# Score tiles 0 and 1 in one pair of PSUM banks, reciprocals transposed from 128 columns, and their 1e-9 added by GpSimd

## The chip, the cores and the metric

One core of a Trainium2 chip. The metric is the time of one execution on the device in microseconds, the median of a few runs. Another 0.5% (some 5 us) is about what a measurement of this kernel can tell from no change.

## The reference, cut to what matters

An attention with forgetting gates feeds two feed-forward networks. Only the attention is touched: batch 4, 8 heads, 576 positions, 64 values a head.

```python
scores = scale * np.matmul(q, k.transpose(0, 1, 3, 2))
cum = np.cumsum(np.log(np.clip(f, 0.0001, 1.0)), axis=-1)
scores = np.where(causal, -1e9, scores + cum[:, :, :, None] - cum[:, :, None, :])
attn = np.exp(scores - np.max(scores, axis=-1, keepdims=True))
attn = attn / (np.sum(attn, axis=-1, keepdims=True) + 1e-09)
x = np.matmul(attn, v)
```

## The kernel before

The work of the attention goes by pairs of heads, 16 of them. Every product is made of two fp32r parts (h and l) of each factor. The steps of a pair `p`, with their engines:

- `load_q`, `load_k`, `load_v`, `decay_rows`: DMAs of SyncE. `qh`, `kh`, `ql`, `kl`, `v_high`, `v_low`: GpSimd makes the two parts.
- `scores` i (TensorE, i = 0 to 4): the score tiles of 128 rows, four terms each. Tiles 0 to 3 use 64 rows of the array for each head, both heads side by side, each head into a bank of its own (tag "s", two banks in all); a tile of fewer than 256 columns is made 256 wide. Tile 4 has both heads in one tile on 128 rows (tag "X").
- `minimum` t (VectorE, t = 0 to 8, tile i and 8 - i being the two heads of score tile i): reads the scores from PSUM, adds the mask, writes them to the tile P and gives the row's extreme. `exp` t (ScalarE): the exponential in place, with the row's sum.
- `transposes` g (TensorE, g = 0 to 6): 25 blocks of P, two to four in a bank (tag "t", two banks in all). `evac_h` g (ScalarE) and `evac_l` g (VectorE) take the two parts out.
- `rinv` (VectorE): adds 1e-9 to the nine sums of a row (line 280) and takes the reciprocal (line 281). `rinv_t` (TensorE, also tag "t") transposes the nine columns, `rinv_b` (ScalarE) copies them out, `rinv_c` and `rinv_d` (SyncE) send them to DRAM and spread them over the partitions.
- `pv` (TensorE, line 324), `out_a` (ScalarE), `out_b` (VectorE), `out_c` (GpSimd, times the reciprocal), `out_d` (SyncE).

The order is written out by hand. `WHEN` gives each step a due time in units of a plan; pair p adds 9 p to it, the first pair uses `START` and the last `END`; `run` sorts all steps by due time and emits them in that order, and every engine executes its own in the order of emission. So the order on an engine is read by taking the due times modulo 9. A tile's buffer is reused in the order in which the tiles are made: the next tile waits until the readers of the one before in that buffer are done. Between the steps stand those of `Weights.op` (list `STEPS`), which prepare the weights of the next layer: one in three or fewer units on VectorE (`SHIFT`, `LOW`, `SIGN`), most of them at 3.294 modulo 9, from the middle on some at 6.381. After the attention come the two networks, in which TensorE has no idle time that matters.

Modulo 9 the parts of the order that the change meets are, before it:

- TensorE: `pv` 0 4, 0 3, 0 1, 1 0, 1 2, `scores` 1, `transposes` 2, 3, `pv` 1 4, 1 3, 1 1, `scores` 0, `rinv_t`, `transposes` 5, 4, `scores` 2, `pv` 0 0, `scores` 4, `pv` 0 2, `transposes` 6, `scores` 3, `transposes` 0, 1.
- VectorE: `minimum` 3, 5, `rinv`, `evac_l` 0, 1, `minimum` 1, 7, a step of `Weights`, `evac_l` 2, 3, `minimum` 0, 8, `out_b` 0, 1, `minimum` 6, `evac_l` 5, `minimum` 2, `evac_l` 4, `minimum` 4, `evac_l` 6.
- ScalarE: `evac_h` 0, 1, `exp` 3, 5, `out_a` 0, `evac_h` 2, 3, `out_a` 1, `rinv_b`, `exp` 7, `evac_h` 5, 4, `exp` 0, 1, 4, 2, `evac_h` 6, `exp` 6, 8.

Of the kernel before, what the change touches and what calls it, by code (L numbers as in the profile page):

```python
# [9 lines left out]
F32 = mybir.dt.float32  # L10
# [3 lines left out]
ALU = mybir.AluOpType  # L14
# [7 lines left out]
class Attention:  # L22
# [59 lines left out]
    def constants(self):  # L82

        nc, c, S = self.nc, self.c, self.S
        self.qrs = [c.tile([128, 640], F32, name=f"qr{i}") for i in range(2)]
        for q in self.qrs:
            nc.gpsimd.memset(q[0:64, 576:640], 0.0)
            nc.gpsimd.memset(q[64:128, 512:576], 0.0)
        self.nbs = [c.tile([128, S], F32R, name=f"nb{i}") for i in range(2)]
        nc.gpsimd.memset(self.nbs[0][64:128].bitcast(F32), 0.0)  # L90

        self.one = c.tile([128, 256], F32R, name="one")
        o = self.one[:].bitcast(F32)
        nc.gpsimd.memset(o, 0.0)
        for r, t in ((0, 128), (64, 192)):
            nc.gpsimd.memset(o[r:r + 2, 0:128], 1.0)
            nc.gpsimd.memset(o[r:r + 2, t:t + 64], 1.0)

        self.mask = c.tile([128, 512], F32, name="mask")
        nc.gpsimd.memset(self.mask, 0.0)  # L100
        nc.gpsimd.affine_select(self.mask, self.mask, pattern=[[-1, 512]], compare_op=ALU.is_ge,
                                fill=-8e9, base=384, channel_multiplier=1)
        self.mask4 = c.tile([128, S], F32, name="mask4")
        self.eps = c.tile([128, 9], F32, name="eps")
        nc.gpsimd.memset(self.eps, 1e-9)

    def constants2(self):
        nc, c, S = self.nc, self.c, self.S
        nc.gpsimd.memset(self.mask4, 0.0)
        for i in range(2):  # L110
            M = self.mask4[64 * i:64 * i + 64]
            nc.gpsimd.affine_select(M, M, pattern=[[-1, S]], compare_op=ALU.is_ge, fill=-8e9, base=512,
                                    channel_multiplier=1)
        nc.gpsimd.memset(self.nbs[1][:].bitcast(F32), 0.0)
        ident = c.tile([128, 128], F32, name="ident")
        nc.gpsimd.memset(ident, 0.0)
        nc.gpsimd.affine_select(ident, ident, pattern=[[-1, 128]], compare_op=ALU.not_equal,
                                fill=1.0, base=0, channel_multiplier=1)
# [74 lines left out]
    def v_low(self, R, p):  # L193
        self.sub(("v_low",), R["V"][:, :, :, 1], R["vr"].rearrange("p j (h e) -> p j h e", h=2), R["V"][:, :, :, 0])

    def scores(self, R, p, i):


        nc, S = self.nc, self.S
        Xh, Xl, Yh, Yl, nb = R["Xh"], R["Xl"], R["Yh"], R["Yl"], self.nbs[p % 2]  # L200
        if "P" not in R:
            R["P"] = self.pp.tile([128, sum(self.W9)], F32, tag="P", name=f"P{p}")
            R["m"] = self.sm.tile([128, 9], F32, tag="m", name=f"m{p}")
            R["sum"] = self.sm.tile([128, 9], F32, tag="sum", name=f"sum{p}")
        n = 4
        if i == 4:
            ps = self.ps.tile([128, 1024], F32, tag="X", name=f"s{p}_4")
            for c in range(2):
                for j, (L, r) in enumerate(((Xh[:, 512:640], Yh), (Xl[:, 512:640], Yh), (Xh[:, 512:640], Yl),
                                            (self.one[:, 128:256], nb))):  # L210
                    nc.tensor.matmul(ps[:, 224 + 288 * c:512 + 288 * c], L, r[:, 288 * c:288 * c + 288],
                                     start=j == 0, stop=j == n - 1)
            R["src", 4] = R["P"], ps[:, 224:800], self.mask4
            return
        w = self.W9[i]
        N = max(w, 256)
        ps = [self.ps.tile([128, 512], F32, tag="s", bufs=2, name=f"s{p}_{i}_{h}") for h in range(2)]
        q = slice(128 * i, 128 * i + 128)
        for j, (L, r) in enumerate(((Xh[:, q], Yh), (Xl[:, q], Yh), (Xh[:, q], Yl), (self.one[:, 0:128], nb))):
            for h in range(2):  # L220
                o = slice(64 * h, 64 * h + 64)
                nc.tensor.matmul(ps[h][:, 0:N], L[o], r[o, 0:N], start=j == 0, stop=j == n - 1)  # L222
        for h in range(2):
            R["src", (i, 8 - i)[h]] = R["P"], ps[h][:, 0:w], self.mask[:, 512 - w:512]

    def minimum(self, R, p, t):
        P, src, mask = R["src", t]
# [46 lines left out]
            self.nc.vector.tensor_sub(l, s, h)  # L274


    def rinv(self, R, p):
        nc = self.nc
        r = self.sm.tile([128, 9], F32, tag="r", name=f"r{p}")
        nc.vector.tensor_add(r, R["sum"], self.eps)  # L280
        nc.vector.reciprocal(r, r)
        R["r"] = r

    def rinv_t(self, R, p):
        ps = self.ps.tile([128, 512], F32, tag="t", bufs=2, name=f"rt{p}")
        self.nc.tensor.transpose(ps[0:9, 0:128], R["r"], self.ident)
        R["rt"] = ps

    def rinv_b(self, R, p):
# [54 lines left out]
    def out_d(self, R, p):  # L344
# [13 lines left out]
        ("load_q",): -23.5799, ("load_k",): -16.9757, ("qh",): -11.2698, ("kh",): -9.873, ("ql",): -9.3162,  # L358
        ("kl",): -9.0904, ("decay_rows",): -8.1126, ("scores", 4): -2.7503, ("scores", 3): -2.135,
        ("minimum", 4): -2.019, ("minimum", 3): -0.0192, ("minimum", 5): 0.3552, ("scores", 1): 2.0404,  # L360
        ("exp", 3): 2.9766, ("exp", 5): 3.066, ("minimum", 1): 3.0798, ("minimum", 7): 3.2918, ("scores", 0): 4.02,
        ("minimum", 0): 4.7488, ("minimum", 8): 4.7664, ("exp", 7): 4.9241, ("scores", 2): 5.5069,
        ("minimum", 6): 5.8865, ("exp", 0): 6.2356, ("minimum", 2): 6.379, ("exp", 1): 6.6423, ("exp", 4): 6.7033,
        ("exp", 2): 7.105, ("transposes", 0): 7.5695, ("load_v",): 7.7728, ("exp", 6): 7.8053,
        ("transposes", 1): 7.9929, ("exp", 8): 8.7191, ("evac_h", 0): 9.5166, ("evac_h", 1): 9.5706,
        ("rinv",): 10.083, ("v_high",): 10.1126, ("evac_l", 0): 10.4436, ("v_low",): 10.514,
        ("evac_l", 1): 11.2219, ("transposes", 2): 12.2269, ("evac_h", 2): 12.276, ("transposes", 3): 12.3519,
        ("evac_h", 3): 12.4099, ("evac_l", 2): 13.0431, ("rinv_t",): 13.1193, ("rinv_b",): 13.2113,
        ("evac_l", 3): 13.7368, ("transposes", 5): 13.8096, ("transposes", 4): 13.9726, ("evac_h", 5): 14.8574,
        ("pv", 0, 0): 14.9016, ("evac_h", 4): 14.9515, ("evac_l", 5): 15.137, ("pv", 0, 2): 15.291,  # L370
        ("evac_l", 4): 15.6663, ("transposes", 6): 15.699, ("evac_h", 6): 16.5991, ("evac_l", 6): 16.839,
# [3 lines left out]
        ("out_b", 0): 22.9328, ("out_b", 1): 23.1796, ("out_c",): 27.9509, ("out_d",): 29.0433}  # L375
    START = {
        ("scores", 1): -93.1054, ("minimum", 7): -76.489, ("minimum", 1): -61.3588, ("load_v",): -51.5282,
        ("scores", 4): -51.4691, ("scores", 0): -44.2927, ("minimum", 4): -43.1442, ("minimum", 0): -42.9929,
        ("exp", 1): -39.9503, ("minimum", 8): -34.2473, ("exp", 4): -33.3442, ("scores", 2): -33.1312,
        ("minimum", 6): -32.9417, ("minimum", 2): -30.1161, ("exp", 0): -27.5664, ("v_high",): -26.4226,  # L380
        ("exp", 8): -25.5812, ("scores", 3): -25.0262, ("exp", 7): -15.5786, ("exp", 6): -14.3123,
# [4 lines left out]
        ("evac_l", 0): 4.0423, ("evac_l", 5): 4.5113, ("transposes", 6): 6.9606, ("evac_h", 6): 7.9405,  # L386
        ("transposes", 2): 8.6556, ("evac_h", 2): 9.5839, ("pv", 0, 0): 10.1568, ("pv", 0, 4): 10.8868,
        ("evac_l", 6): 11.2953, ("evac_l", 2): 12.6569, ("transposes", 4): 13.0223, ("pv", 0, 2): 13.1329,
        ("evac_h", 4): 13.5619, ("rinv",): 13.795, ("evac_l", 4): 14.2703, ("rinv_t",): 15.9595,
        ("rinv_b",): 16.8417, ("pv", 0, 3): 18.6967, ("pv", 0, 1): 19.0591, ("rinv_c",): 19.3907,  # L390
        ("pv", 1, 0): 19.9842, ("pv", 1, 4): 20.0606, ("pv", 1, 3): 20.5574, ("pv", 1, 2): 21.0619,
        ("pv", 1, 1): 21.6901, ("out_a", 0): 22.1074, ("out_a", 1): 22.8142, ("out_b", 0): 22.9613,
# [3 lines left out]
        ("kl",): -7.3377, ("ql",): -3.7962, ("load_v",): -3.2787, ("scores", 4): -2.3475, ("minimum", 4): -2.1479,  # L396
        ("scores", 3): -1.8482, ("minimum", 5): 0.0327, ("minimum", 3): 0.4621, ("exp", 5): 0.5894,
        ("exp", 4): 2.234, ("scores", 1): 2.774, ("minimum", 1): 2.8564, ("minimum", 7): 3.1801,
        ("scores", 0): 4.1802, ("minimum", 8): 5.1018, ("exp", 3): 5.8442, ("minimum", 0): 5.8642,
        ("scores", 2): 6.4249, ("exp", 1): 6.5503, ("exp", 7): 7.1358, ("minimum", 6): 7.8256, ("exp", 6): 8.5445,  # L400
        ("minimum", 2): 10.9888, ("exp", 0): 12.1987, ("exp", 2): 12.2247, ("transposes", 0): 14.1161,
        ("evac_h", 0): 14.7614, ("exp", 8): 14.8228, ("transposes", 2): 15.3451, ("evac_l", 0): 15.8926,
        ("v_high",): 16.9288, ("evac_h", 2): 17.1908, ("transposes", 1): 18.0963, ("evac_h", 1): 18.3091,
        ("evac_l", 2): 19.0513, ("rinv",): 19.0903, ("transposes", 4): 19.1493, ("evac_l", 1): 19.2978,
        ("rinv_t",): 22.2139, ("evac_h", 4): 22.6115, ("rinv_b",): 24.2699, ("evac_l", 4): 25.904,
        ("rinv_c",): 27.1176, ("v_low",): 27.3115, ("transposes", 3): 27.4876, ("evac_h", 3): 29.2544,
        ("transposes", 5): 29.4306, ("evac_l", 3): 31.4099, ("evac_h", 5): 32.5541, ("transposes", 6): 32.9931,
# [142 lines left out]
class Moe1:  # L550
# [12 lines left out]
    def hidden(self, u, pieces):  # L563
        nc, ch, W = self.nc, self.chain, self.W
        t, fc = divmod(u, self.FC)
        N = self.TILES[t][1]
        (wh, wl), (xh, xl) = self.W.done[f"wi{fc}"], self.x.parts[t]
        ph = self.ps.tile([128, 512], F32, tag="s", bufs=2, name=f"h{u}")[:, 0:N]
        three(nc, ph, [(block(wh, c), block(wl, c), xh[:, c], xl[:, c]) for c in range(4)], True, True)
# [566 lines left out]
```

## Time and profile before

| | |
|---|---|
| median of 3 runs | 1052.52 us (1050.94 to 1055.83) |
| span of the profiled execution | 1054.0 us |
| TensorE, VectorE, ScalarE, GpSimd busy, share of the span | 97%, 64%, 43%, 14% |
| the attention's steady part, pairs 3 to 15 | 44.31 to 189.02 us |

The profiled execution lies 1.5 us over the median and within the runs. A timeline's row gives the start in us from the start of the span, the length in us, the engine, the line of the kernel, the operation, the tiles it writes and reads, shapes, and how many like it follow one another; in brackets stands how long the engine was idle before and who ended that.

### The profile page before, as it was taken

The page shows a single profiled execution, that of the slowest core. Times are in us where ns is not written, and L with a number is a line of the kernel's source. Part 1 is how long each engine was busy: PE and PEld are TensorE (multiplying, and loading weights), DVE is VectorE, ACT ScalarE, POOL GpSimd, SP SyncE. Part 2 cuts the span into 40 slices and gives each one's busy share as a digit, 9 for nine tenths or more (in the row PEclk, how much of TensorE's full clock was granted, in tenths as well). Part 3 has the DMA queues.
Part 4 walks back from the last instruction along what each step waited for, and adds up shares of the span by engine and source line. Part 5 has one row for each costly group of instructions (what it writes and reads, how often), then busy time and mean ns, then how long its engine had stood idle before and what let it go on. Part 6 is the DMA issues. An engine that isn't in the chain of part 4 may idle for free.

```text
span 1054.0 us, 17893 instructions
## 1 busy us (share of the span) xinstructions
PE 1026.4 (97%) x6376; PEld 920.1 (87%) x6376; DVE 673.7 (64%) x1454; ACT 454.6 (43%) x989; POOL 152.8 (14%) x158
## 2 busy tenths in 40 slices
PE   5999999899999999999999999999999999999998
PEld 4788788678889999999999998999999899899997
DVE  5899999879927646646646556655655655555421
ACT  4889888866634443444434432222221222221121
POOL 7667777520000000000000000000000000000000
PEclk8999999999999999999999999999999999999999
DMA  5355454555525646646644699987887887696481
GB/s 146 113 143 155 138 159 139 132 160 185 211 80 210 225 155 216 218 156 213 221 155 157 204 375 353 355 302 240 278 264 231 288 263 231 227 295 209 142 277 60
DMA packets 129492, 218.23 MB, mean 207 GB/s; under 512 B 16174, under 2 KB 46526, under 8 KB 129404
## 3 DMA queue, kind: packets, MB, share of 16 engines
q1 hardware_dynamic: 126316, 212.01, 61.4%
q10 hardware_dynamic: 3088, 5.09, 1.4%
q8 instruction: 50, 0.82, 0.3%
q14 instruction: 38, 0.31, 0.1%
HBM read 171.21 MB, written 45.83 MB: 206 GB/s over the span
## 4 chain that ended last, share of the span: by engine, by line
PE 91%; DVE 5%; ACT 2%; DMA 1%; issue 1%; SPq 0%; POOL 0%; ACTq 0%; DVEq 0%
PE h L542 7%; PE h L543 7%; PE h L541 7%; PE x L324 4%; PE s L222 4%; PE t L252 4%; PE h_S L543 4%; PE h_S L541 4%; PE h_S L542 4%; PE h_A L541 3%; PE h_A L543 3%; PE h_A L542 3%; PE oY L542 3%; PE zX L902 3%; PE oY L541 3%; PE oY L543 3%
## 5 line engine op out<-in xcount | busy, mean ns | idle before, releaser
L543 PE MATMUL h<-xh,wi_l 128*128 128x448 f32 (+1 forms) x320 | 119.0, 372 | 0.0
L542 PE MATMUL h<-xl,wi_h 128*128 128x448 f32 (+1 forms) x320 | 119.0, 372 | 0.0
L541 PE MATMUL h<-xh,wi_h 128*128 128x448 f32 (+1 forms) x320 | 118.9, 372 | 0.0
L583 DVE TENSOR_TENSOR gl<-L,gh 128x448 fp32r<-128x448 f32 (+1 forms) x80 | 51.0, 638 | 102.5 <-ACT gh L582 102.3
L571 ACT ACTIVATE L<-h 128x448 f32<-128x448 f32 (+1 forms) x80 | 44.3, 554 | 147.9 <-PE h L543 144.1
L878 ACT CAST gh<-bl 128x512 fp32r<-128x512 f32 (+1 forms) x60 | 34.7, 579 | 168.9 <-DVE bl L849 141.8
L234 ACT ACTIVATE P<-P,m 128x128 f32<-128x128 f32 (+3 forms) x144 | 83.2, 581 | 9.4 <-DVE m L229 9.1
L542 PE MATMUL h_S<-x,ring 128*128 128x256 f32 x288 | 81.5, 283 | 0.0
L229 DVE CUSTOM_DVE_ANT_0 P<-s,mask 128x256 f32<-128x256 f32 (+3 forms) x144 | 70.6, 516 | 10.6 <-PE s L222 5.9
L541 PE MATMUL h_S<-x,ring 128*128 128x256 f32 x264 | 74.7, 283 | 0.0
L543 PE MATMUL h_S<-x,ring 128*128 128x256 f32 x264 | 74.7, 283 | 0.0
L252 PE MATMUL t<-ident,P 128*128 128x128 f32 x400 | 61.4, 287 | 7.3 <-DVE PTbl L274 3.5
L542 PEld LDWEIGHTS h<-xl,wi_h 128*128 128x128 f32 x320 | 60.1, 188 | 7.2
L541 PEld LDWEIGHTS h<-xh,wi_h 128*128 128x128 f32 x320 | 60.1, 188 | 7.2
L543 PEld LDWEIGHTS h<-xh,wi_l 128*128 128x128 f32 x320 | 60.1, 188 | 7.0
L683 DVE TENSOR_TENSOR l<-fw,sh 128x512 fp32r<-128x512 f32 x60 | 40.8, 686 | 36.8 <-ACT sh L682 36.5
L847 ACT ACTIVATE bh<-bh 128x1024 f32<-128x1024 f32 x24 | 25.4, 1060 | 88.9 <-DVE bh L845 88.9
L252 PEld LDWEIGHTS t<-ident,P 128*128 128x128 f32 x400 | 44.7, 144 | 21.4 <-DVE PTbl L274 5.3
L542 PEld LDWEIGHTS h_S<-x,ring 128*128 128x128 f32 x288 | 55.3, 192 | 0.0
L835 DVE TENSOR_TENSOR L<-h_S,L 128x256 f32<-128x256 f32 x48 | 20.3, 423 | 53.7 <-PE h_S L543 50.6
L542 PE MATMUL h_A<-x,ring 128*128 128x256 f32 x192 | 54.3, 283 | 0.0
L879 DVE TENSOR_TENSOR gl<-bl,gh 128x512 fp32r<-128x512 f32 (+1 forms) x60 | 38.0, 635 | 24.9 <-ACT gh L878 24.9
(235 smaller groups left out, 3061.3 us busy)
## 6 DMA issues: line engine op xcount, KB each, us to landing
ring<-sd_g SPq DMA_DIRECT2D x192, 256.0 KB
ring<-sd_v SPq DMA_DIRECT2D x192, 256.0 KB
raw_wi<-in_moe_w_in_dram SPq DMA_DIRECT2D x16, 512.0 KB
raw_wo<-in_moe_w_out_dram SPq DMA_DIRECT2D x16, 512.0 KB
fraw<-in_moe_w_gate_dram SPq DMA_DIRECT2D x12, 512.0 KB
fraw<-in_moe_w_out_dram SPq DMA_DIRECT2D x12, 512.0 KB
sd_g<-sh SPq DMA_DIRECT2D x24, 256.0 KB
sd_g<-l SPq DMA_DIRECT2D x24, 256.0 KB
```

The lines of the kernel that those rows point to most:

```text
L222: nc.tensor.matmul(ps[h][:, 0:N], L[o], r[o, 0:N], start=j == 0, stop=j == n - 1)
L229: self.nc.vector.tensor_tensor_reduce(P, src, mask, -0.125, 3e38, op0=ALU.add, op1=ALU.min, accum_out=R["m"][:, t:t + 1])
L234: self.nc.scalar.activation(P, P, AF.Exp, bias=R["m"][:, t:t + 1], scale=-1.0, accum_out=R["sum"][:, t:t + 1])
L252: nc.tensor.transpose(ps[:, 128 * n:128 * n + 128], R["P"][:, o:o + 128], self.ident)
L324: nc.tensor.matmul(R["acc%d" % h][:, o:o + n], v, t[:, col:col + n], start=j == 0 and w == 0, stop=j == 1 and w == 1)
L541: nc.tensor.matmul(ps, ah, bh, start=start and i == 0, stop=False)
L542: nc.tensor.matmul(ps, ah, bl, start=False, stop=False)
L543: nc.tensor.matmul(ps, al, bh, start=False, stop=stop and i == n - 1)
L571: nc.scalar.activation(g, ph, AF.Softplus)
L583: nc.vector.tensor_sub(gl, s, gh)
L683: nc.vector.tensor_sub(l, w[n], h)
L879: nc.vector.tensor_sub(l, s, h)
```

## The change

Four things. `scores` 1 makes tile 1 and, right behind it, tile 0, in the same two banks: tile 1 in columns 0 to 255, tile 0 in columns 256 to 511; the step `scores` 0 is gone. The addition of 1e-9 becomes a step of its own on GpSimd, `rinv_a`, due at 10.6 (after `v_low`). The reciprocals are written into one of two standing tiles of 128 columns, which are zeroed once, and all 128 columns are transposed; the tile `eps` is gone. And three steps get other due times: `rinv` from 10.083 to 14.6 (modulo 9: behind `out_b` 1, ahead of `minimum` 6), `rinv_t` from 13.1193 to 15.69 (behind `pv` 0 2, ahead of `transposes` 6), `rinv_b` from 13.2113 to 15.695 (behind `exp` 1, ahead of `exp` 4).

```diff
-        self.eps = c.tile([128, 9], F32, name="eps")
-        nc.gpsimd.memset(self.eps, 1e-9)
...
+        self.rs = [c.tile([128, 128], F32, name=f"r{i}") for i in range(2)]
+        for t in self.rs:
+            nc.gpsimd.memset(t, 0.0)
...
+    SAME = {1: (1, 0)}
...
-        w = self.W9[i]
-        N = max(w, 256)
         ps = [self.ps.tile([128, 512], F32, tag="s", bufs=2, name=f"s{p}_{i}_{h}") for h in range(2)]
-        q = slice(128 * i, 128 * i + 128)
-        for j, (L, r) in enumerate(((Xh[:, q], Yh), (Xl[:, q], Yh), (Xh[:, q], Yl), (self.one[:, 0:128], nb))):
+        for k in self.SAME.get(i, (i,)):
+            w = self.W9[k]
+            N = max(w, 256)
+            a = 256 if k != i else 0
+            q = slice(128 * k, 128 * k + 128)
+            for j, (L, r) in enumerate(((Xh[:, q], Yh), (Xl[:, q], Yh), (Xh[:, q], Yl), (self.one[:, 0:128], nb))):
+                for h in range(2):
+                    o = slice(64 * h, 64 * h + 64)
+                    nc.tensor.matmul(ps[h][:, a:a + N], L[o], r[o, 0:N], start=j == 0, stop=j == n - 1)
             for h in range(2):
-                o = slice(64 * h, 64 * h + 64)
-                nc.tensor.matmul(ps[h][:, 0:N], L[o], r[o, 0:N], start=j == 0, stop=j == n - 1)
-        for h in range(2):
-            R["src", (i, 8 - i)[h]] = R["P"], ps[h][:, 0:w], self.mask[:, 512 - w:512]
+                R["src", (k, 8 - k)[h]] = R["P"], ps[h][:, a:a + w], self.mask[:, 512 - w:512]
...
+    def rinv_a(self, R, p):
+        R["e"] = self.sm.tile([128, 9], F32, tag="r", name=f"e{p}")
+        self.nc.gpsimd.tensor_scalar(R["e"], R["sum"], 1e-9, 1.0, op0=ALU.add, op1=ALU.mult)
+
     def rinv(self, R, p):
-        nc = self.nc
-        r = self.sm.tile([128, 9], F32, tag="r", name=f"r{p}")
-        nc.vector.tensor_add(r, R["sum"], self.eps)
-        nc.vector.reciprocal(r, r)
-        R["r"] = r
+        R["r"] = self.rs[p % 2]
+        self.nc.vector.reciprocal(R["r"][:, 0:9], R["e"])
 
     def rinv_t(self, R, p):
...
-        self.nc.tensor.transpose(ps[0:9, 0:128], R["r"], self.ident)
+        self.nc.tensor.transpose(ps[:, 0:128], R["r"], self.ident)
...
-        ("rinv",): 10.083, ("v_high",): 10.1126, ("evac_l", 0): 10.4436, ("v_low",): 10.514,
+        ("rinv",): 14.6, ("v_high",): 10.1126, ("evac_l", 0): 10.4436, ("v_low",): 10.514,
...
-        ("evac_h", 3): 12.4099, ("evac_l", 2): 13.0431, ("rinv_t",): 13.1193, ("rinv_b",): 13.2113,
+        ("evac_h", 3): 12.4099, ("evac_l", 2): 13.0431, ("rinv_t",): 15.69, ("rinv_b",): 15.695, ("rinv_a",): 10.6,
```

In `START` and `END` the entry of `scores` 0 goes and one of `rinv_a` comes (0.6 and 16.0); nothing else changes there.

## Rows read from the trace of the kernel before

**Rows 1.** Busy time by stretch: us, then each engine with its instructions, granted clock, DMA.
```profile
44.31:114.58 70.27, 70.27 (x567) 59.10 (x566) 68.12 (x189) 62.96 (x181) 50.10 (x45) 1.00 0.52 143
114.58:189.02 74.44, 71.68 (x569) 59.26 (x567) 72.63 (x193) 64.72 (x185) 53.84 (x46) 1.00 0.55 155
```

**Rows 2.** Timeline of TensorE (start, us long): first matmul of score tile 4, pairs 3 and 15.
```profile
44.31 0.29 PE L211 MATMUL s<-Yh,Xh 128*128 128x288 f32 x1
...
189.02 0.29 PE L211 MATMUL s<-Yh,Xh 128*128 128x288 f32 x1
```

**Rows 3.** Timeline of ScalarE in one period: exponentials and copies.
```profile
80.03 0.77 ACT L234 ACTIVATE P<-P,m 128x576 f32<-128x576 f32 x1
80.79 0.60 ACT L234 ACTIVATE P<-P,m 128x384 f32<-128x384 f32 x1
...
81.69 0.61 ACT L234 ACTIVATE P<-P,m 128x384 f32<-128x384 f32 x1
...
82.30 0.39 ACT L234 ACTIVATE P<-P,m 128x128 f32<-128x128 f32 x1
...
88.97 0.26 ACT L291 COPY rt_sb<-rt 9x128 f32<-9x128 f32 x1 [0.24 <-PE rt L286]
89.13 0.50 ACT L234 ACTIVATE P<-P,m 128x256 f32<-128x256 f32 x1
```

**Rows 4.** Timeline of TensorE in the same period.
```profile
79.45 0.29 PE L211 MATMUL s<-Yh,Xh 128*128 128x288 f32 x1
...
80.81 0.38 PE L252 MATMUL t<-ident,P 128*128 128x128 f32 x2
...
82.24 1.09 PE L252 MATMUL t<-ident,P 128*128 128x128 f32 x8
...
83.09 0.28 PE L324 MATMUL x<-PTbh,V 128*128 128x64 f32 x1
...
85.09 0.39 PE L222 MATMUL s<-Yh,Xh 64*128 64x256 f32 x2
85.31 0.28 PE L222 MATMUL s<-Yh,Xl 64*128 64x256 f32 x2
...
85.54 0.28 PE L222 MATMUL s<-nb,one 64*128 64x256 f32 x2
...
88.80 1.02 PE L252 MATMUL t<-ident,P 128*128 128x128 f32 x7
...
89.75 0.44 PE L222 MATMUL s<-Yh,Xh 64*128 64x384 f32 x2
...
90.65 0.54 PE L324 MATMUL x<-PTah,V 128*128 128x256 f32 x2
...
91.30 0.29 PE L211 MATMUL s<-Yh,Xh 128*128 128x288 f32 x1
```

**Rows 5.** Timeline of VectorE in the same period.
```profile
83.57 1.39 DVE L280 TENSOR_TENSOR r<-sum,eps 128x9 f32<-128x9 f32 x1
...
85.13 1.23 DVE L274 TENSOR_TENSOR PTal<-t,PTah 128x512 fp32r<-128x512 f32 x2
...
86.28 0.41 DVE L229 CUSTOM_DVE_ANT_0 P<-s,mask 128x256 f32<-128x256 f32 x1
...
...
86.96 0.59 DVE L487 TENSOR_SCALAR w_wi<-w_wi 128x512 uint32<-128x512 uint32 x1
87.47 1.27 DVE L274 TENSOR_TENSOR PTbl<-t,PTbh 128x512 fp32r<-128x512 f32 x2
```

**Rows 6.** Timeline of GpSimd in the same period.
```profile
83.49 1.45 POOL L342 TENSOR_TENSOR xs<-xs,rb 128x576 f32<-128x576 f32 x1
...
85.72 1.55 POOL L170 TENSOR_TENSOR V<-vr,V 128x640 fp32r<-128x640 f32 x1
```

**Rows 7.** One line of the kernel, the addition of eps: durations ns min/median/max, first and last start.
```profile
L280 DVE TENSOR_TENSOR r<-sum,eps x16: 167/934/1392, 31.8 to 206.9; 128x9 f32<-128x9 f32 x16
```

**Rows 8.** Timeline of the DMA queue of SyncE: the store of the reciprocals.
```profile
81.76 0.44 SPq L295 DMA_DIRECT2D rd<-rt_sb  x1
```

More of the change, by code (lines that the diff above doesn't have):

```diff
@@ L360 @@
         ("minimum", 4): -2.019, ("minimum", 3): -0.0192, ("minimum", 5): 0.3552, ("scores", 1): 2.0404,
-        ("exp", 3): 2.9766, ("exp", 5): 3.066, ("minimum", 1): 3.0798, ("minimum", 7): 3.2918, ("scores", 0): 4.02,
-        ("minimum", 0): 4.7488, ("minimum", 8): 4.7664, ("exp", 7): 4.9241, ("scores", 2): 5.5069,
+        ("exp", 3): 2.9766, ("exp", 5): 3.066, ("minimum", 1): 3.0798, ("minimum", 7): 3.2918,         ("minimum", 0): 4.7488, ("minimum", 8): 4.7664, ("exp", 7): 4.9241, ("scores", 2): 5.5069,
         ("minimum", 6): 5.8865, ("exp", 0): 6.2356, ("minimum", 2): 6.379, ("exp", 1): 6.6423, ("exp", 4): 6.7033,
@@ L377 @@
         ("scores", 1): -93.1054, ("minimum", 7): -76.489, ("minimum", 1): -61.3588, ("load_v",): -51.5282,
-        ("scores", 4): -51.4691, ("scores", 0): -44.2927, ("minimum", 4): -43.1442, ("minimum", 0): -42.9929,
+        ("scores", 4): -51.4691, ("minimum", 4): -43.1442, ("minimum", 0): -42.9929,
         ("exp", 1): -39.9503, ("minimum", 8): -34.2473, ("exp", 4): -33.3442, ("scores", 2): -33.1312,
@@ L388 @@
         ("evac_l", 6): 11.2953, ("evac_l", 2): 12.6569, ("transposes", 4): 13.0223, ("pv", 0, 2): 13.1329,
-        ("evac_h", 4): 13.5619, ("rinv",): 13.795, ("evac_l", 4): 14.2703, ("rinv_t",): 15.9595,
+        ("evac_h", 4): 13.5619, ("rinv",): 13.795, ("rinv_a",): 0.6, ("evac_l", 4): 14.2703, ("rinv_t",): 15.9595,
         ("rinv_b",): 16.8417, ("pv", 0, 3): 18.6967, ("pv", 0, 1): 19.0591, ("rinv_c",): 19.3907,
@@ L398 @@
         ("exp", 4): 2.234, ("scores", 1): 2.774, ("minimum", 1): 2.8564, ("minimum", 7): 3.1801,
-        ("scores", 0): 4.1802, ("minimum", 8): 5.1018, ("exp", 3): 5.8442, ("minimum", 0): 5.8642,
+        ("minimum", 8): 5.1018, ("exp", 3): 5.8442, ("minimum", 0): 5.8642,
         ("scores", 2): 6.4249, ("exp", 1): 6.5503, ("exp", 7): 7.1358, ("minimum", 6): 7.8256, ("exp", 6): 8.5445,
@@ L403 @@
         ("v_high",): 16.9288, ("evac_h", 2): 17.1908, ("transposes", 1): 18.0963, ("evac_h", 1): 18.3091,
-        ("evac_l", 2): 19.0513, ("rinv",): 19.0903, ("transposes", 4): 19.1493, ("evac_l", 1): 19.2978,
+        ("evac_l", 2): 19.0513, ("rinv",): 19.0903, ("rinv_a",): 16.0, ("transposes", 4): 19.1493, ("evac_l", 1): 19.2978,
         ("rinv_t",): 22.2139, ("evac_h", 4): 22.6115, ("rinv_b",): 24.2699, ("evac_l", 4): 25.904,
```

## The prediction

> **What bounds the kernel now.** I read the busy shares by slice first: behind the attention TensorE is busy all the time, so whatever the attention loses or wins arrives at the end whole. Then the stretches of the steady attention [rows 1]. Twelve periods, each from one score tile 4 to the next, take 144.71 us [rows 2]; the first six 70.27, which is 11.71 each, the last six 74.44, 12.41 each. In the first TensorE shows no idle time at all and VectorE 68.12 of 70.27, so the two run in step and neither has room; ScalarE has (70.27 - 62.96) / 6 = 1.22 us of room in a period. The .70 that a late period costs more goes with the second weight step that VectorE gets there. Last I read the timelines of one period, 79.45 to 91.30, engine by engine [rows 3 to 6]: with all engines this full, the change has to be followed along the order in which each engine executes.
>
> **Parts that cost or bring little.** The addition on VectorE takes .17 to 1.39 us for nine columns, .93 as a rule [rows 7]; in the period read it lasted from 83.57 to 84.96 [rows 5], and ended where GpSimd's `out_c` ended, 83.49 + 1.45 = 84.94 [rows 6]. So it mostly waits, and VectorE gets about 1 us a period back. On GpSimd the new addition stands behind `v_low`, which ends at 85.72 + 1.55 = 87.27 [rows 6]; the sums are complete from `exp` 8 on, that is 82.7 [rows 3]. The reciprocal is now due behind `out_b` 1 and ahead of `minimum` 6, which needs `scores` 2 of 89.75 [rows 4], so over 2 us later: I cost the addition at nothing. No row shows nine columns on GpSimd; between .17 (VectorE's least [rows 7]) and 1.55 (640 columns [rows 6]) all of it fits into that cover, and where it didn't VectorE would wait with `minimum` 6, `evac_l` 5 and all behind them. A transposition of 128 columns is a step of (83.09 - 82.24) / 8 = .106 [rows 4], no dearer than others. The store of the reciprocals left SyncE at 81.76 [rows 8], behind a load; the copy in its new place ends at about 81.4 (below), so that queue isn't held. The standing tiles are cleared once, before the first pair.
>
> **TensorE's gain.** The first of the four row pairs of a 64-row group takes 85.31 - 85.09 = .22, the others (85.54 - 85.31) / 2 = .115 [rows 4]. Ahead of such a group, between transpositions and scores, lies .95 - 7 x .106 = .21 without work (88.80 to 89.75). One group fewer saves the extra .105 and some of such a gap: .1 to .3 a period.
>
> **The new waits.** First, `minimum` 1. It stood behind `rinv`, `evac_l` 0 and 1 and started at 86.28 [rows 5], 1.19 after `scores` 1 started [rows 4]. Now the scores it reads lie in a bank into which tile 0 is still written. I take it that it waits for the last of these: .45 (85.09 to 85.54) + 4 x .115 + .28 (the last one's length) + .05 (hand-over, as between 87.47 + 1.27 and 88.80) = 1.24 after the start. No row of before shows an engine reading a bank while TensorE writes another part of it, so the wait for tile 0 is between 0 and 4 x .115 = .46. I take .46. So what the addition gives VectorE back is spent waiting here, with `minimum` 7, the weight step and `evac_l` 2 and 3 queued behind: they come no earlier after the scores than now.
>
> The Trainium skill (PSUM — Partial Sum Buffer, PSUM bank collisions raise a hardware error) says that two engines must be kept apart on one bank even at different addresses. By it the .46 is there whatever the columns, and the rule speaks against this half of the change; no run here shows it yet, and without it the sum would be the one with 0.
>
> Second, `rinv_b` on ScalarE. It needs `rinv_t`, which TensorE now reaches where `transposes` 6 stood, at 80.81 [rows 4]. ScalarE is through with `exp` 1 at 80.03 and would begin `exp` 4 there [rows 3]. It now has to wait for the transposition: .27 (a pair of them takes .38, one step of .106 less) + .05 = 81.13, then .16 for the copy (88.97 to 89.13 [rows 3]): `exp` 4 starts at 81.29, 1.26 late. Behind it are queued `exp` 2, `evac_h` 6, `exp` 6, which together took 80.03 to 82.30 = 2.27 [rows 3]; `exp` 6 is now done at 83.56. `transposes` 1 needs it, and would be due on TensorE four steps after 82.24, at 82.67. It had .37 to spare, now TensorE waits .94. ScalarE's room of 1.22 doesn't help, since the wait comes from TensorE itself: when TensorE is late, so is `rinv_t`.
>
> **The sum.** So there is a closed loop through three engines, and its length is the new period. From `rinv_t`: transposition and hand-over .32; `rinv_b` .16; ScalarE to the end of `exp` 6 and hand-over 2.32; `transposes` 1, four steps, .43; the products up to the scores, 83.09 to 85.09, 2.00; scores 1 and 0 and hand-over 1.24; `minimum` 1 and 7, 86.28 to 86.96, .68; the weight step .51 (to 87.47); `evac_l` 2 and 3 and hand-over, to 88.80, 1.33; `transposes` 4, three steps and the gap, .32 + .21 = .53 (it needs `evac_l` 3; 5 needs only 2); `scores` 2, 89.75 to 90.65, .90; `pv` 0 0 to 91.30, .65; `scores` 4 and `pv` 0 2, 79.45 to 80.81, 1.36. Sum 12.43 [rows 3 to 5].
>
> Against 11.71 that is .72 more. In the late periods the second weight step stands on VectorE ahead of `evac_l` 4, which `transposes` 6 now has to wait for (it took the buffer of 5, now it takes that of 4), so I leave their extra .70 on top: again .72 more. Twelve periods and about one more for both ends, whose own orders only half follow this: 13 x .72 = 9.4 us. The profiled execution would go from 1054.0 to 1063.4; it stands 1.5 above the median, so from the median 1052.5 + 9.4 = 1062.
>
> Bounds: without the wait for tile 0, -13 x .46 = -6.0; the late periods' .70 swallowed by the loop, -6 x .70 = -4.2; a weight step of the longer kinds and five more hand-overs, up to +.4 in each of 13 loops, +5.2. Not all at once, that is 1056 to 1067.
>
> **The rivals.** (1) The wait is covered: the .94 is gone if TensorE reaches `rinv_t` about 1 us earlier against ScalarE than I place it. Then the loop is 12.43 - .94 = 11.49, under the 11.71 now, and at most 13 x .22 = 2.9 is gained: 1050 to 1054 with some of the wait left. For it speaks ScalarE's room, against it that ScalarE waits for `rinv_t` even now (.24 [rows 3]) and that nothing of the change puts TensorE ahead at that place. (2) Faster: both reliefs arrive. VectorE's 1 us takes away what the late periods cost more, 6 x .70 = 4.2, and TensorE's .3 comes 13 times, 3.9: 1044.4. It needs both waits not to bind: `minimum` 1 not behind tile 0, `rinv_b` not behind TensorE. VectorE's 97% speak for it, the two orders against. (3) Worse: the waits add up beyond one loop, `transposes` 6 stalling for `evac_l` 4 as well as `transposes` 1 for `exp` 6 in every period, another .5 each, 6.5 in all: 1069. It decides from the point where VectorE comes to `evac_l` 4 later than ScalarE to `exp` 6. (4) The addition isn't off the path: the reciprocal waits for GpSimd because GpSimd is held by its own waits for weights. It has over 2 us of cover; beyond that each period pays the difference, as in (3).
>
> **How the numbers follow.** Forecast .70, (1) .14, (2) .09, (3) .05, (4) .02. Half a per cent, 5.3 us, is about what a measurement of this kernel can tell from no change, so (1) counts as the same and all else but (2) as slower: .77 slower, .14 the same, .09 faster. The range takes the forecast's own, the upper end for (3) and (4), and that half of (1) which lies next to the forecast: 1052 to 1069. Left out are (2) and half of (1), .16.
>
> **What would show it.** In the profile after: periods of about 12.4 us where 11.7 stood, and about 13.1 later; ScalarE idle about 1 us in each period ahead of `rinv_b`, with TensorE's transposition named; TensorE idle ahead of `transposes` 1, with `exp` 6 named; VectorE idle ahead of `minimum` 1, with the scores named, over 1 us; VectorE's work less by about 1 us a period. Wrong would be: no idle time of ScalarE at `rinv_b` (then rival 1 or 2), `minimum` 1 starting before tile 0 is written (the smaller sum), or a loss that lies behind the attention.

## The result and the profile after

The changed kernel takes 1066.26 us (median of 4 runs, 1062.9 to 1067.2), the kernel before 1051.95 (4 runs, 1050.94 to 1055.83): ratio 1.0127, 95% interval 1.0108 to 1.0146, so 1.3% slower. The profiled execution has a span of 1064.7 us against 1054.0, 10.7 more. In every run here that has both, the span is some 1.8 us (once 2.1) shorter than the time of the same execution; so the profile before belongs to the execution of 1055.83, the slowest of its four, 3.9 over their median and not 1.5 as I wrote ahead of the prediction. Between the medians the change costs 14.3 us, and the profiles account for 10.7 of them.

The stretches from pair 3 to 9 and from 9 to 15, as in [rows 1]:

```profile
48.15:123.17 75.02, 72.40 (x566) 58.56 (x565) 62.15 (x181) 62.39 (x181) 51.20 (x51) 1.00 0.48 135
123.17:199.50 76.33, 72.67 (x568) 58.90 (x567) 66.04 (x186) 63.65 (x183) 55.15 (x53) 1.00 0.52 146
```

A period is 75.02 / 6 = 12.50 us early and 76.33 / 6 = 12.72 late, where 11.71 and 12.41 stood. VectorE works 6 us less in six periods; TensorE, which was never idle early on, now is for 2.62 us. Against before, score tile 4 of pair 3 is 48.15 - 44.31 = 3.84 us late, the six early periods add 4.75, the six late ones 1.89, and all behind them .2 (865.2 from the last of these points to the end, 865.0 before). In the runs below that rest varies between 861 and 866 us, whatever the kernel, so periods and starts tell more than spans.

The waits between 44 and 200 us that bear on the change (engine, what it was to write and its line, what it waited for and its line: us in total, times, longest; PEld is TensorE's loading of weights), first before, then after. Others, among them longer ones of GpSimd, are left out:

```profile
ACT rt_sb L291 <- PE rt L286: 2.9, 11, 0.4
```
```profile
DVE P L234 <- PE s L227: 14.8, 12, 1.3
ACT rt_sb L297 <- PE rt L292: 13.6, 12, 1.7
PEld t L257 <- DVE PTbl L279: 11.4, 40, 1.0
PEld t L257 <- ACT rt_sb L297: 6.4, 12, 0.5
PE t L257 <- ACT rt_sb L297: 4.1, 12, 0.3
```

The first of after has no counterpart before: `minimum` 1 waits for the scores. Nor have the last two: `transposes` 6 wait for the copy of the reciprocals. One period shows each place. TensorE, 85.65 to 98.11, the lines that answer to [rows 4]:

```profile
85.65 0.30 PE L214 MATMUL s<-Yh,Xh 128*128 128x288 f32 x1
...
87.06 0.30 PE L292 MATMUL rt<-ident,r 128*128 128x128 f32 x1
87.70 0.44 PE L257 MATMUL t<-ident,P 128*128 128x128 f32 x2 [0.34 <-ACT rt_sb L297]
88.07 0.50 PE L227 MATMUL s<-Yh,Xh 64*128 64x512 f32 x2
...
89.20 1.36 PE L257 MATMUL t<-ident,P 128*128 128x128 f32 x8
90.31 0.28 PE L330 MATMUL x<-PTbh,V 128*128 128x64 f32 x1
...
92.30 0.39 PE L227 MATMUL s<-Yh,Xh 64*128 64x256 f32 x2
...
92.76 0.29 PE L227 MATMUL s<-nb,one 64*128 64x256 f32 x2
...
93.23 0.29 PE L227 MATMUL s<-nb,one 64*128 64x256 f32 x2
93.45 1.09 PE L257 MATMUL t<-ident,P 128*128 128x128 f32 x8
...
95.50 1.14 PE L257 MATMUL t<-ident,P 128*128 128x128 f32 x7
96.58 0.44 PE L227 MATMUL s<-Yh,Xh 64*128 64x384 f32 x2
...
97.47 0.53 PE L330 MATMUL x<-PTah,V 128*128 128x256 f32 x2
...
98.11 0.30 PE L214 MATMUL s<-Yh,Xh 128*128 128x288 f32 x1
```

VectorE, ScalarE and GpSimd there, for [rows 5], [rows 3] and [rows 6]:

```profile
87.30 0.55 DVE L279 TENSOR_TENSOR PTbl<-t,PTbh 128x384 fp32r<-128x384 f32 x1
...
93.54 0.42 DVE L234 CUSTOM_DVE_ANT_0 P<-s,mask 128x256 f32<-128x256 f32 x1 [1.28 <-PE s L227]
...
94.24 0.42 DVE L492 TENSOR_SCALAR w_wi<-w_wi 128x512 uint32<-128x512 uint32 x1
94.76 1.29 DVE L279 TENSOR_TENSOR PTbl<-t,PTbh 128x512 fp32r<-128x512 f32 x2
```
```profile
87.39 0.25 ACT L297 COPY rt_sb<-rt 9x128 f32<-9x128 f32 x1 [0.86 <-PE rt L292]
...
89.22 0.61 ACT L239 ACTIVATE P<-P,m 128x384 f32<-128x384 f32 x1
```
```profile
92.08 1.57 POOL L171 TENSOR_TENSOR V<-vr,V 128x640 fp32r<-128x640 f32 x1
93.73 0.20 POOL L284 TENSOR_SCALAR e<-sum 128x9 f32<-128x9 f32 x1
```

`minimum` 1 starts .02 us after tile 0's last product (93.23 + .29 = 93.52), not after tile 1's (93.05). The copy makes ScalarE wait .86, and TensorE .34 behind it; `exp` 6 ends at 89.22 + .61 = 89.83, and `transposes` 1, the second four of the eight steps at 89.20, start at about 89.89. GpSimd's addition of nine columns takes .20 and nobody waits for it. SyncE's store of the reciprocals [rows 8] starts at 87.67, right behind the copy.

### The profile page after: what moved, and what is told of

It is laid out like the page before. It is cut to its first block, busy times and chain, and to the rows that moved or that the text cites. A ratio compares the mean times of both kernels' runs of the same rounds, so it can differ in the third digit from the quotient of the medians.

```text
span 1064.7 us, 17905 instructions
## 1 busy us (share of the span) xinstructions
PE 1031.4 (97%) x6376; PEld 921.4 (87%) x6376; DVE 659.6 (62%) x1438; ACT 453.0 (43%) x989; POOL 156.1 (15%) x175
## 4 chain that ended last, share of the span: by engine, by line
PE 88%; DVE 6%; ACT 3%; issue 1%; DMA 1%; SPq 0%; ACTq 0%; DVEq 0%
PE h L548 7%; PE h L546 7%; PE h L547 7%; PE h_S L548 4%; PE h_S L546 4%; PE h_S L547 4%; PE s L227 4%; PE x L330 4%; PE t L257 3%; PE h_A L546 3%; PE h_A L548 3%; PE h_A L547 3%; PE oY L547 3%; PE zX L907 2%; PE oY L546 2%; PE oY L548 2%
## 5 line engine op out<-in xcount | busy, mean ns | idle before, releaser
L239 ACT ACTIVATE P<-P,m 128x128 f32<-128x128 f32 (+3 forms) x144 | 83.2, 579 | 10.8 <-DVE m L234 10.6
L257 PE MATMUL t<-ident,P 128*128 128x128 f32 x400 | 65.2, 291 | 11.7 <-ACT rt_sb L297 4.8
```

Source lines behind the costliest of these rows:

```text
L239: self.nc.scalar.activation(P, P, AF.Exp, bias=R["m"][:, t:t + 1], scale=-1.0, accum_out=R["sum"][:, t:t + 1])
L257: nc.tensor.transpose(ps[:, 128 * n:128 * n + 128], R["P"][:, o:o + 128], self.ident)
```

## TensorE's period, piece by piece

Each piece is the difference of two starts on TensorE's timeline of one early period (the period that begins at 91.30 before, at 85.65 after; one period of each experiment in the same way; that of e2 is one of its two long ones, its other early periods take 12.62 to 12.72), in us:

| piece | before | after | e2 move only | e4 copy later | e8 changed, weights first | e1 merge only | e11 cover back |
|---|---|---|---|---|---|---|---|
| `scores` 4, `pv` 0 2 | 1.35 | 1.41 | 1.93 | 1.40 | 1.40 | 1.36 | 1.36 |
| (`rinv_t`) and `transposes` 6 | .31 | 1.01 | .98 | 1.28 | 1.01 | .31 | .31 |
| `transposes` 0, 1 | .85 | 1.11 | 1.11 | .85 | 1.11 | .85 | .97 |
| `scores` 1 and 0 | 1.33 | 1.15 | 1.33 | 1.14 | 1.15 | 1.15 | 1.15 |
| (`rinv_t`) and `transposes` 5, 4 | 1.10 | 1.08 | .92 | 1.07 | 1.07 | 1.51 | 1.42 |
| all else | 6.70 | 6.70 | 6.69 | 6.69 | 6.72 | 6.71 | 6.61 |
| period | 11.64 | 12.46 | 12.96 | 12.43 | 12.46 | 11.89 | 11.82 |

After against before: the scores one behind the other save .18; the transposition in its new place with the wait behind it costs .70; `transposes` 0 and 1 cost .26 more, since 1 waits for `exp` 6; .06 and -.02 are left: .82 in all. `rinv_t` is gone from the fifth piece (.16), but `transposes` 4 wait there for `evac_l` 3 (.14).

## The experiments

**One part alone.** First the scores alone (e1: `scores` 1 makes tile 0 too, all else as before), then the new places alone (e2), then the addition alone on GpSimd, ahead of `out_c`, with the reciprocal due at 11.5 (e3). The edit of e2, abridged:

```diff
-        ("rinv",): 10.083 ... ("rinv_t",): 13.1193, ("rinv_b",): 13.2113
+        ("rinv",): 14.6   ... ("rinv_t",): 15.69,   ("rinv_b",): 15.695
```

> The kernel before with score tiles 0 and 1 merged and nothing else: the addition stays on VectorE, the reciprocal and its transposition stay in their old places, nine columns wide. Theory of the loop (the loss of the changed kernel is ScalarE waiting for the transposed reciprocals, tied to minimum 1 waiting for tile 0): the loop loses its ScalarE part, from the first matmul of scores 1 to scores 2 it is 1.24 + .68 + .51 + 1.33 + .95 = 4.71 us against 4.66 in the kernel before, so periods of 11.7 to 12.0 us, 12.2 to 12.5 late, 1 to 5 us over the kernel before: 1053 to 1057. Rival, the bank (minimum 1 waiting for tile 0 carries nearly the whole loss): periods near 12.4, 1062 to 1066. Either way VectorE shows little idle time ahead of minimum 1, since the addition stands before it.

> The kernel before with the three due times of the change and nothing else: tiles 0 and 1 apart, the addition on VectorE (now behind out_b 1), nine columns. Theory of the loop: ScalarE waits for the transposition about .9 us a period ahead of exp 4, TensorE .3 to 1 us ahead of transposes 6 and 1; VectorE keeps its 1 us of additions, so nothing is given back: 12.4 to 13.1 us a period, 1062 to 1070. Rival, the bank: no wait for tile 0 here, so 1050 to 1054.

> The kernel before with the addition of 1e-9 as a GpSimd step of its own (ahead of out_c) and the reciprocal behind evac_l 1; tiles 0 and 1 apart, transposition and copy in their old places, nine columns. If VectorE bounds the period beside TensorE (its 97%), its about 1 us is worth .1 to .3 us in an early period and up to .7 in a late one: 2 to 6 us under the kernel before, 1046 to 1050. If TensorE alone bounds it, within 1 us of the kernel before.

| | periods early, late | pair 3's tile 4 | us (median) | ratio to before |
|---|---|---|---|---|
| before | 11.71, 12.41 | 44.31 | | |
| changed | 12.50, 12.72 | 48.15 | 1066.26 | 1.0127 (1.0108 to 1.0146) |
| e1 merge only | 11.95, 12.54 | 46.26 | 1060.93 | 1.0067 (1.0045 to 1.0089) |
| e2 move only | 12.74, 12.93 | 44.31 | 1065.72 | 1.0105 (1.008 to 1.0129) |
| e3 add only | 11.99, 12.40 | 44.45 | 1055.27 | 1.001 (.999 to 1.003) |

The new places alone cost +1.03 us an early period, more than the whole change (+.79):

```profile
44.31:120.75 76.44, 72.87 (x567) 58.89 (x566) 65.37 (x186) 63.24 (x183) 50.34 (x45) 1.00 0.47 132
```

They don't have the scores' .18 and leave the addition on VectorE, which may be why; in the period of the table `rinv_t` waits .41 there for an `evac_l`. The scores alone cost .24 an early period, as the loop's theory had it, and 1.95 at the start, which was not in it: their total lies above the range of that theory and below that of the rival. That the shared bank does nearly all of the harm falls with e2, which shares none and is as slow within the noise. The 128 columns in place of nine were not tried alone.

e3 is the same as the kernel before within the noise, and its early periods are .28 longer, which I had not expected. In its trace VectorE's microsecond is spent twice: VectorE waits for the scores, and then its weight step runs beside GpSimd's `v_low` (86.83 to 88.38) and takes .98, where the step of [rows 5], beside GpSimd for its first .31, took .59:

```profile
86.99 0.42 DVE L229 CUSTOM_DVE_ANT_0 P<-s,mask 128x256 f32<-128x256 f32 x1 [0.88 <-PE s L222]
87.34 0.42 DVE L229 CUSTOM_DVE_ANT_0 P<-s,mask 128x256 f32<-128x256 f32 x1
87.68 0.98 DVE L488 TENSOR_SCALAR w_wi<-w_wi 128x512 uint32<-128x512 uint32 x1
```
```profile
86.83 1.55 POOL L170 TENSOR_TENSOR V<-vr,V 128x640 fp32r<-128x640 f32 x1
```

**The copy a little later.** If ScalarE's wait holds the period, `exp` 4 and 2 ahead of the copy should free it.

```diff
-        ("rinv_b",): 15.695
+        ("rinv_b",): 16.3
```

> The changed kernel with one due time changed: the copy rinv_b at 16.3 in place of 15.695, which puts it on ScalarE behind exp 2 in place of ahead of exp 4. Theory of the loop: exp 4 and exp 2 (1.36 us) run while the transposition is made, ScalarE's .9 us of waiting goes to below .1 and the period falls from 12.5 to about 11.8 us, late ones to 12.0 to 12.4: 1054 to 1059. Rival, the bank: the wait for tile 0 stays, so 1063 to 1067 as the changed kernel.

1063.93 us, ratio 1.0102 (1.0064 to 1.014), periods 12.50 and 12.84: ScalarE's wait is gone, and nothing is won. My theory missed; the time is that of the rival, but e5 below shows that the wait for tile 0 doesn't hold the period by itself. TensorE now waits in the same place, longer, for something else:

```profile
86.97 0.30 PE L292 MATMUL rt<-ident,r 128*128 128x128 f32 x1
87.91 0.41 PE L257 MATMUL t<-ident,P 128*128 128x128 f32 x2 [0.64 <-DVE PTbl L279]
```
```profile
87.21 0.55 DVE L279 TENSOR_TENSOR PTbl<-t,PTbh 128x384 fp32r<-128x384 f32 x1
```

`transposes` 6 begin .15 us after `evac_l` 4 is done (87.76). With the copy ahead of them in the order of emission they take the buffer of `rinv_t`: in the changed kernel they start at 87.70, while `evac_l` 4 lasts until 87.85. With the copy behind them they take the buffer of 4. So a tile does not always get the buffer that the order of making would give, as I had written of the kernel; by which rule it gets one, no run here settles (in the changed kernel `evac_l` 4 is due ahead of the copy, so it isn't simply the first release in the order of emission). `transposes` 1 no longer wait (.85), and the table's second and third piece together are 2.13 against 2.12. The edit takes one route away and, by the other buffer, brings in a second of the same length; so e4 doesn't show what the copy's place alone costs.

**The old places, with the other parts left in (e5); pair 0 apart (e7).** In e5 `rinv_t` and `rinv_b` have their old due times; `rinv` and the addition stand as in e3.

```diff
-        ("rinv",): 14.6, ("rinv_a",): 10.6, ("rinv_t",): 15.69,   ("rinv_b",): 15.695
+        ("rinv",): 11.5, ("rinv_a",): 9.93, ("rinv_t",): 13.1193, ("rinv_b",): 13.2113
```

> The changed kernel with the reciprocal's steps put back to where they stood before the change: tiles 0 and 1 one behind the other, the 128-column reciprocal sums and GpSimd's addition stay, but the transposition of the reciprocal and its copy no longer stand between transposes 4 and transposes 6. Theory (two loops of equal length, one by way of ScalarE's copy and one by way of the buffer that the reciprocal's transposition takes right ahead of transposes 6): both go together, early periods 11.9 to 12.0 us, late ones 12.4 to 12.55, as where tiles 0 and 1 alone were put together; 1057 to 1062 us. Rival (minimum 1's wait for tile 0 holds the period by itself, wherever the reciprocal stands): early periods stay at 12.4 or more, 1063 to 1067 us.

> The changed kernel, in which pair 0 alone keeps tiles 0 and 1 apart as before the change. If the 3.84 us by which the changed kernel starts its periods later come from the first pair's tiles, score tile 4 of pair 3 starts at 44.5 to 46.5 us instead of 48.15, with periods of 12.5 and 12.7 us as in the changed kernel, and 1 to 3 us less in all. If they come from the clock or from pairs 1 and 2, it stays at 47.5 to 48.5 us.

e5: 1063.36 us, ratio 1.0078 (1.0054 to 1.0103), a little over the range that I gave; periods 12.02 and 12.52, as the theory had them. So the new places account for .48 of an early period on top of the other parts, and the rival falls by the periods, though the time lies at its lower end:

```profile
47.95:120.07 72.12, 69.82 (x566) 58.99 (x565) 62.10 (x183) 63.27 (x182) 51.52 (x51) 1.00 0.51 139
```

The start is as late as in the changed kernel (47.95); the profiled execution, 1060.64, lies in the range, so this doesn't explain why the median is over it. e7: one run of 1064.3, periods 12.50 and 12.72 as in the changed kernel, start 45.36, which is 2.79 earlier.

But the start is not pair 0's alone. The stretch from 32 to 40 us, first the changed kernel (and its part from 35 to 38), then e8 below, which has the same merged pair 0 and starts its periods at 44.93, then e7:

```profile
32.00:40.00 8.00, 6.56 (x36) 4.88 (x36) 5.37 (x21) 4.74 (x17) 4.95 (x5) 0.79 0.14 40
35.00:38.00 3.00, 3.00 (x13) 2.52 (x14) 1.61 (x5) 1.92 (x6) 2.95 (x4) 0.50 0.26 71
```
```profile
32.00:40.00 8.00, 8.00 (x65) 6.54 (x66) 6.76 (x19) 6.15 (x20) 6.56 (x6) 1.00 0.29 79
32.00:40.00 8.00, 7.63 (x62) 6.17 (x62) 5.74 (x20) 6.09 (x19) 6.19 (x6) 1.00 0.29 77
```

TensorE's wait for an `evac_l` at that place, in the changed kernel, in e7 and in e1:

```profile
33.69 0.41 PE L330 MATMUL x<-PTbl,V 128*128 128x320 f32 x1 [1.44 <-DVE PTbl L279]
```
```profile
32.37 0.41 PE L332 MATMUL x<-PTbl,V 128*128 128x320 f32 x1 [1.41 <-DVE PTbl L281]
```
```profile
32.78 0.41 PE L328 MATMUL x<-PTbl,V 128*128 128x320 f32 x1 [1.42 <-DVE PTbl L278]
```

In the changed kernel the granted clock is .79 there: .50, the lower level of 1.2 GHz, from 35 to 38 us, behind the wait of 1.44 us, and 1.00, 2.4 GHz, before and after. e4 and e5 also have the wait of 1.44 and .79 there and start at 48.06 and 47.95; every other kernel with the merged scores has 1.00 there and starts between 44.9 and 46.3, with pair 0 merged or not. The wait alone doesn't decide it: e7 and e1 have nearly the same one, 1.41 and 1.42, and keep 1.00, and no run shows what does decide. By an estimate, a mean of .79 between 1 and .5 is .42 of 8 us at the lower level, about 1.7 us of work lost; from the end of the wait to tile 4 of pair 3 the changed kernel takes 14.46 us and e7 12.99. So of the 3.84 some 1.5 to 1.7 go with the clock, and the rest with the first pairs' own orders, which no run takes apart further.

**The weight step ahead of `minimum` 1**, in the kernel with the addition alone (e6), in the changed kernel (e8), and in e5 (e9); e10 is e9 with pair 0 apart.

```diff
-STEPS = [(-7.81, 0), (1.294, 1), (3.294, 2), (12.294, 3), ...
+STEPS = [(-7.81, 0), (1.294, 1), (2.994, 2), (11.994, 3), ...
```

> The kernel with GpSimd's addition alone, and VectorE's weight step of each pair one place earlier, ahead of minimum 1 instead of behind it. Theory (the microsecond that VectorE saved was lost twice, in waiting for scores 1 and in a weight step slowed down beside GpSimd's work): the weight step fills the wait, early periods 11.4 to 11.7 us, 1046 to 1051 us. Rival (TensorE's own order bounds the period, and VectorE's time is free there): early periods 11.7 or more, 1052 to 1054 us, as before.

> The changed kernel with one edit: VectorE's weight step of each pair stands ahead of minimum 1 instead of behind minimum 7. By the sum of the prediction the weight step (.42 to .69 us here) is a term of the closed loop, and minimum 1 waits 1.28 us for the scores, so that the step fits into the wait. If the loop is what sets the period, early periods shrink by about that term, from 12.50 to 11.9 to 12.1 us, unless ScalarE's copies ahead of evac_l 2 give back some of it; 1056 to 1061 us. Rival (the loops close without VectorE's minimum 1, over the transposition, its copy and ScalarE alone): early periods stay at 12.4 to 12.5, 1063 to 1067 us.

> The changed kernel with the reciprocal's steps in their old places (early periods 12.02 us) and, besides, the weight step ahead of minimum 1. If tiles 0 and 1 one behind the other give TensorE .1 to .3 us a period, and only the waits at minimum 1 hid it, early periods come to 11.4 to 11.6 us, under the 11.68 that the kernel with tiles apart and the weight step first had. If they give TensorE nothing, early periods are 11.65 us or more. The start stays late (score tile 4 of pair 3 at 47 to 48 us).

> As the kernel with the reciprocal's steps in their old places and the weight step ahead of minimum 1, and pair 0 alone with tiles 0 and 1 apart. Expected: the periods of that kernel, and a start 2.5 to 3 us earlier, since pair 0's tiles apart brought 2.79 us in the changed kernel. If the periods are 11.4 to 11.6 us, 1048 to 1052 us in all; if they are 11.7 or more, 1052 to 1056 us.

| | periods early, late | pair 3's tile 4 | us | ratio to before |
|---|---|---|---|---|
| e6 add only, weights first | 11.68, 12.15 | 43.35 | 1052.01 | .9989 (.9969 to 1.0009) |
| e8 changed, weights first | 12.45, 12.54 | 44.93 | 1059.85 | 1.0061 (1.0046 to 1.0076) |
| e9 old places, weights first | 11.89, 12.37 | 45.69 | 1054.83 (one run) | |
| e10 as e9, pair 0 apart | 11.89, 12.36 | 45.01 | 1054.47 | 1.0012 (.9993 to 1.0032) |

e6 gives back the .3 that e3 had lost, but its total is the rival's; its early period, 11.68, lies at the edge of the theory's range and is no clear gain on 11.71. e8 contradicts my expectation: its total is in the range, its early period isn't. The step was taken out of the loop, `minimum` 1 waits .95 instead of 1.28, the period moves by .05, and `evac_l` 2 waits for ScalarE instead:

```profile
88.79 0.41 DVE L492 TENSOR_SCALAR w_wi<-w_wi 128x512 uint32<-128x512 uint32 x1
90.16 0.42 DVE L234 CUSTOM_DVE_ANT_0 P<-s,mask 128x256 f32<-128x256 f32 x1 [0.95 <-PE s L227]
...
91.37 1.29 DVE L279 TENSOR_TENSOR PTbl<-t,PTbh 128x512 fp32r<-128x512 f32 x2 [0.44 <-ACT PTbh L275]
```

e9 takes the worse of its two expectations: 11.89, not 11.6 or less. The starts are misses too: I had put that of e9 at 47 to 48, and that of e10 2.5 to 3 us earlier than e9's; they are 45.69 and 45.01.

**The cover.** In e1 and e9 it is the fifth piece that lost, 1.10 to 1.51: TensorE waits ahead of `rinv_t` and `transposes` 5 for `evac_l` of 2 and 3, here in e1:

```profile
91.58 0.98 PE L256 MATMUL t<-ident,P 128*128 128x128 f32 x7 [0.32 <-DVE PTbl L278]
```

Tile 0's scores (.66 us) used to lie between `transposes` 2, 3 and 5, and covered that evacuation. e11 puts `scores` 2 there, in e9.

```diff
-  ("minimum", 0): 4.7488, ("minimum", 8): 4.7664, ("scores", 2): 5.5069, ("rinv_t",): 13.1193, ("rinv_b",): 13.2113
+  ("minimum", 0): 3.3,    ("minimum", 8): 3.31,   ("scores", 2): 4.6,    ("rinv_t",): 13.9,    ("rinv_b",): 13.99
```

> The kernel with tiles 0 and 1 one behind the other, the reciprocal's steps in their old places and the weight step first (early periods 11.89 us), in which scores 2 now stand ahead of transposes 5 and 4, and minima 0 and 8, which scores 2 have to wait for, right behind minima 1 and 7; the reciprocal's transposition goes between transposes 5 and 4. Theory (tiles 0 and 1 together save TensorE about .2 us a period, and lose more because the .66 us of tile 0's scores no longer lie between transposes 2, 3 and transposes 5, where they covered the evacuation of 2): with scores 2 (.9 us) in that place the wait ahead of transposes 5 is gone, early periods 11.45 to 11.65 us, late ones 12.0 to 12.2; 1048 to 1053 us. Rival (the two scores one behind the other cost TensorE or VectorE something by themselves): early periods stay at 11.8 to 11.9, 1053 to 1057 us.

1055.23 us, ratio 1.0011 (.9992 to 1.0029), periods 11.83 and 11.89. The late periods came down by .48, the early ones by .06 only; early periods and time are those of the rival. The wait ahead of `transposes` 5 is gone, and a known one stands one step on, since I had put `rinv_t` right ahead of `transposes` 4:

```profile
91.44 0.66 PE L257 MATMUL t<-ident,P 128*128 128x128 f32 x4
91.94 0.27 PE L292 MATMUL rt<-ident,r 128*128 128x128 f32 x1
92.55 0.55 PE L257 MATMUL t<-ident,P 128*128 128x128 f32 x3 [0.34 <-ACT rt_sb L297]
```

It is the .34 of the changed kernel again. That the period would be about 11.5 without it is arithmetic, not a run; so the cover explains the wait ahead of 5, the gain of the merged scores in the whole stays unshown, and the rival, that they cost something by themselves, isn't ruled out.

**The second weight step.** In e6 the three late periods with a second weight step take 12.81, 13.13 and 12.05, the others 11.63. e12 puts it beside the first, ahead of `minimum` 1.

```diff
-(87.381, 3), (92.994, 4) ... (105.381, 3), (110.994, 4) ... (123.381, 3), (128.994, 4)
+(92.8, 3),   (92.994, 4) ... (110.8, 3),   (110.994, 4) ... (128.8, 3),   (128.994, 4)
```

> The kernel with GpSimd's addition alone and the weight step ahead of minimum 1 (early periods 11.68, late 12.15 us; three of the late ones, with a second weight step, 12.8 to 13.1). The second weight step now stands there too, 5.4 places later. If VectorE has time there (it still waits .3 us at minimum 1 and .4 us at evac_l 2 in each period), the three long periods come down to 11.7 to 12.2, late periods to 11.65 to 11.9; 1047 to 1051 us. If not, the long periods stay at 12.4 or more and the time at 1050 to 1053 us.

1048.63 us (8 runs, 1046.29 to 1050.64), ratio .9946 (.9926 to .9966): faster than both kernels, by .5% than the one before, with periods of 11.69 and 11.70, as expected. TensorE has no idle time in either stretch:

```profile
43.00:113.00 70.00, 69.99 (x565) 58.86 (x564) 62.70 (x181) 62.91 (x180) 53.76 (x51) 1.00 0.51 142
113.00:183.00 70.00, 70.00 (x567) 59.17 (x566) 66.34 (x187) 63.73 (x182) 55.91 (x52) 1.00 0.57 155
```

So one part of the change, the addition on GpSimd, together with weight steps that stand where VectorE would wait, beats the kernel before. How much of it the addition brings isn't shown: no run moves the weight steps and leaves the addition on VectorE.

## Why the prediction came out right, point by point

- **The loop.** Forecast 12.43, measured 12.46 in the period shown, and leg by leg: from `rinv_t` to `transposes` 1 2.83 (from 87.06 to the second four of the eight steps, 90.31 - 4 x .106 = 89.89; the sum had 2.80), to `scores` 1 2.41 (2.43), to `scores` 2 4.28 (1.24 + .68 + .51 + 1.33 + .53 = 4.29), then .89, .64 and 1.41 (.90, .65, 1.36).
- **What the sum left out** is that it is not the only loop of that length. Neither of the two legs that the runs shortened gave anything back: e4 took the copy out of ScalarE's leg, and `transposes` 6, now in the buffer of 4, were held by `evac_l` 4 for as long; e8 took the weight step out of VectorE's leg, and `evac_l` 2 then waited .44 for `evac_h` 2 of ScalarE. The sum gave the right time for the change and would have given the wrong advice for mending it.
- **Where TensorE waits.** I had all .94 ahead of `transposes` 1. It is .26 there and .34 ahead of `transposes` 6, which take the buffer of `rinv_t` and not that of `transposes` 4. With the .30 of `rinv_t` itself that is .90: right in sum, wrong in place, and the step that failed is "it took the buffer of 5, now it takes that of 4". The sum doesn't hang on it, since the loop runs by ScalarE either way.
- **The late periods.** On that step I had left their extra .70 on top, 13.1. They are 12.72: VectorE now has idle time in each period, and a second weight step costs about .25 (12.70 and 12.71 beside 12.47 and 12.44), where it cost about 1 before (12.82 beside 11.82 and 11.86). Six times .41 is 2.4 us that I had too much. One of the six, 13.20 where 12.17 stood, is long for a reason that the runs don't take apart; in e8 it is 12.43.
- **The start.** I had put one period's .72 there; it is 3.84, which goes in part with the merged scores (1.95 in e1) and in part with a stretch of lower clock. That is 3.1 too little, and it nearly cancels the miss of the late periods, which is luck: 9.4 forecast, 10.7 measured in the profiled executions. The median forecast, 1062, is 4 under the measured 1066: 1.3 of that is the miss between the profiles, the rest comes of the profile before lying so far above its median.
- **`minimum` 1 and tile 0.** I took the whole .46; it is .47 (93.54 against 93.05 + .02). The wait is in the program: `minimum` 0, which reads the other half of the bank, has no wait of its own any more, so that of `minimum` 1 covers both tiles. The Trainium skill (PSUM — Partial Sum Buffer, PSUM bank collisions raise a hardware error) wants just that separation, and the trace agrees with it; what would come of a read without the wait no run here shows. In this kernel the .47 probably costs little by itself: in e8 the .41 of the weight step came out of the same leg and gave .05. No run takes the .47 away.
- **TensorE's gain** of .1 to .3 a period is .18 in the piece itself. What I did not price is the cover that tile 0's scores gave to the evacuation of `transposes` 2 and 3.
- **The additions.** At nothing, as forecast: .20 behind `v_low`, no waits. VectorE's work fell by 1.0 us a period, as forecast, and went into its wait.

## What to carry to other kernels

A step that goes TensorE, ScalarE and back into a buffer that the next TensorE step takes makes TensorE wait for the round trip (.34 us here, in the changed kernel and in e11): look for a place where other TensorE work lies between. Before merging two pieces of an engine's work, ask what the second one covered in its old place. And when one engine's leg of a loop is shortened, look for the route of equal length beside it before counting the gain.

## What I had not expected of the hardware

A weight step on VectorE of one shape (128x512 uint32 in place) took .42 in the changed kernel, with GpSimd idle beside it, .59 in [rows 5], and .98 in e3, most of it beside GpSimd's `v_low`. And a wait of 1.44 us early in three kernels was followed by a stretch at the lower clock, which cost by the estimate above about as much again, while waits of 1.41 and 1.42 at the same place in two others were not.
